# Fused lightning attention and top-1 routing: ranks in the step of the choice, GpSimd's order pinned, four gather buffers, transposed rows copied by ScalarE

## The chip, the core and the metric

The kernel runs on one core of one Trainium2 chip, in float32. The core has TensorE (PE, matrix products and transposes into PSUM), VectorE (DVE), ScalarE (ACT), GpSimd (POOL), and SyncE (SP), which here issues loads and reads. ACT, POOL and SP each have DMA queues of their own; POOL's are the ones with row indices from memory (indirect). The metric is the device time of one execution in microseconds (us), as the median of several runs.

## What is computed

Attention with a decaying state (q, k, v of 4 batches, 8 heads, 768 positions, 64 wide), its output seen as 3072 tokens of 512, then a gate that sends each token to one of 8 experts:

```python
for b in range(nb):                       # blocks of positions
    intra = einsum('bhic,bhjc->bhij', qb, kb) * Dmask
    intra = einsum('bhij,bhjd->bhid', intra, vb)
    inter = einsum('bhid,bhde->bhie', qb * lam_pow, kv_state)
    out[:, :, sl] = intra + inter
    kv_state = lam_block * kv_state + einsum('bhsd,bhse->bhde', kb * rev_pow, vb)
x = out.transpose(0, 2, 1, 3).reshape(B * S, H * D)

expert_idx = argmax(x @ w_gate, axis=1)
gate_w = softmax(x @ w_gate)[arange(N), expert_idx]
for e in range(8):                        # w1[e] is 512x1024, w2[e] 1024x512
    xe = x[expert_idx == e]
    out[expert_idx == e] = gate_w * (maximum(xe @ w1[e], 0) @ w2[e])
```

## The kernel before

**Attention.** Positions go in chunks of 128 (six, n = 0 to 5), batches in pairs, so there are 12 steps (i = 0 to 11, loop at L729); step i works on chunk i // 2. In step i the kernel *leaves* step i - 1, *enters* step i + 1 and *attends* step i. `enter` (L661) issues the loads of the next chunk on SP, transposes q and k on PE, and has POOL form kd = k x decay (L232) for the state. Attending means PE products with the state (L266), the growth of the state (cp, L299, in PSUM bank 4), products with the masked scores (L282); then `update` (L306): POOL forms sd = state x decay (L314), DVE adds cp and sd to the state st (L316). Scores of the next step follow (L242), masked by DVE into mt (L248).

`leave` (L692) turns the finished chunk into rows and gate logits on PE (tx, L324 and L326, in banks 4 to 7), ACT copies both out, and a DMA of ACT's queue writes the rows to xs in device memory. Once all four batches of a chunk are there, `choose` (L336) picks the expert of each token on DVE, as a one-hot tile oh, with running counts ohc. Tokens are thus chosen in groups: groups 0 to 4 are chunks 0 to 4 with four batches, the last chunk makes two groups of two batches. Group n is chosen in step 2n + 2.

**Lists.** `put` (L376) ranks a group's tokens within their experts by two small products on PE (L380), DVE makes slot numbers (slot_i, L389 to L394), and `store` (L395) writes one entry of four numbers for each of 128 tokens by an indirect DMA from POOL (L396); a group of four batches needs four stores. `store_places` (L678) issues up to two stores per group each time it is called. The lists are first filled with an empty entry by a 432 KB DMA from POOL (`empty_lists`, L647), out of the tile `empty`.

**Experts.** A pass works through up to 424 tokens of one expert: its list is read by SP (L421), `fetch` (L440) gathers the rows of xs by indirect DMAs from POOL into tiles xg (L445), `turn` (L468) transposes them on PE (tp, L474, banks 0 and 1) and copies them to xgT, by turns on DVE (L461) and ACT (L459). Pass 0a is the first 256 places of expert 0, taken from chunks 0 to 3 alone, so that it can start ahead of the rest; 0b is the rest of expert 0; passes 1 to 7 follow, one per other expert. Passes 0a and 0b use plain products (L484, L619). The later passes replace eight half-size products by seven, with sums of the operands: of the weights on POOL (s_q, s_k, s_v, w1t in `first_sums`; t_q, t_v, t_k, t_m in `second_sums`, L521 and L524, one pass ahead, in ring buffers of three left by the loads of q, k, v), of the tokens (t_sd, xgT, t_x, t_xT, L514 to L517) and of the hidden values (h_qsT, h_qT, h_kT, h_kd, L507 to L510) on DVE; their products are L560 and L588. The last tiles of a pass, those that don't fit the halved form, go through L619. `scatter` (L451) writes results by indirect DMAs from POOL.

**Order.** A scheduling layer places instructions on each engine's queue and sets the waits between engines; `pin` (L198) keeps an instruction in program order among those pinned. Before the change, kd, sd and the stores are not pinned. Each queue runs in order: an instruction that waits holds what stands behind it on its engine. Tiles from a pool with `bufs=n` rotate through n buffers, and a new tile waits until the last reader of the one n tiles ago is done.

Of the kernel before, what the change touches and what calls it, by code (L numbers as in the profile page):

```python
# [10 lines left out]
F32 = mybir.dt.float32  # L11
BF16 = mybir.dt.bfloat16
I32 = mybir.dt.int32
AX = mybir.AxisListType
ALU = mybir.AluOpType
# [6 lines left out]
def kernel(  # L22
# [29 lines left out]
    nc = tc.nc  # L52
    B, H, S, D = q.shape
    N, MD = out.shape
    E = moe_w_gate.shape[1]
    F = moe_w1.shape[2]
    P = 128
# [13 lines left out]
    R = N + EARLY + P  # L71
    ENTRY = 4
# [3 lines left out]
    const = ctx.enter_context(tc.tile_pool(name="const", bufs=1))  # L76
# [74 lines left out]
    for h in itertools.chain(range(0, H, 2), range(1, H, 2)):  # L151
        nc.vector.tensor_tensor_scan(
            out=decay[:, h % 2, h // 2, :], data0=lam_bc[:, h:h + 1].to_broadcast([P, C]),
            data1=ident, initial=0.0, op0=ALU.mult, op1=ALU.add)

    kdec = const.tile([P, H], F32, name="kdec")
# [28 lines left out]
    ffn = ctx.enter_context(tc.tile_pool(name="ffn", bufs=2))  # L185
# [3 lines left out]
    def bank(i, shape, name):  # L189
        return ps.tile(shape, F32, tag=f"bank{i}", name=name)  # L190
# [7 lines left out]
    def pin(inst):  # L198
        tc.keep_in_program_order(inst)
# [4 lines left out]
    def turned(src, s, t):  # L204
        for i, b in itertools.product(range(HP // 2), range(2)):
            h = s * HP + 2 * i
            pin(nc.tensor.transpose(t[:, i, b, :], src[:, b, h:h + 2, :], ident))
        return t
# [13 lines left out]
    def turn_k(m, s):  # L222
        shp = turned_shape
        tk = turned(m.k, s, bank(2 * s + 1, shp, "tk"))
        kT = work.tile(shp, F32, tag="kT", name="kT")
        nc.scalar.copy(kT, tk)
        m.kT.append(kT)
        if m.n < NSTEP - 1:
            shp = [P, 2, HP, D]
            kd = work.tile(shp, F32, tag="kd", name="kd")  # L230
            hs = slice(s * HP, (s + 1) * HP)
            nc.gpsimd.tensor_tensor(out=kd, in0=m.k[:, :, hs],  # L232
                                    in1=kdec[:, hs].unsqueeze(1).unsqueeze(3).to_broadcast(shp),
                                    op=ALU.mult)
            m.kd.append(kd)

    def score(m, s):
# [20 lines left out]
    def attend_begin(m):  # L258
        m.op = [bank(6 + b, [P, HP, C], f"op{b}") for b in range(2)]
# [46 lines left out]
    def update(m):  # L306
        if m.n < NSTEP - 1:
            to = st[:, m.b:m.b + 2]
            if m.n == 0:
                nc.vector.tensor_copy(to, m.cp)  # L310
            else:
                shp = [P, 2, HP, D]
                sd = work.tile(shp, F32, tag="sd", name="sd")
                nc.gpsimd.tensor_tensor(out=sd, in0=to,  # L314
                                        in1=sdec.unsqueeze(1).to_broadcast(shp), op=ALU.mult)
                nc.vector.tensor_add(to, m.cp, sd)  # L316

    def rows(m, b, lg):
# [84 lines left out]

        return store

    empty = ffn.tile([P, E * R // P, ENTRY], I32, tag="xg", name="empty", bufs=2)
    nc.gpsimd.memset(empty, 0)
    nc.gpsimd.memset(empty[:, :, 1], N)

# [18 lines left out]
    def at(m, t):  # L428

        w = m.widths[t]  # L430
        return m.ids[:w, t, 0:1], m.ids[:w, t, 1:2], m.list[:w, t, 2:3]
# [5 lines left out]
    def fetch(m, rows=1 + N):  # L437
        m.xg = []
        for t, w in enumerate(m.widths):
            if t % 2 == 0:  # L440
                m.xg.append(ffn.tile([P, 2, MD], F32, tag="xg", name="xg", bufs=2))
            gather(m.xg[-1][:w, t % 2, :], at(m, t)[0], rows)

    def gather(dst, idx, rows):
        nc.gpsimd.indirect_dma_start(  # L445
            out=dst, out_offset=None, in_=xs[:rows, :],
            in_offset=bass.IndirectOffsetOnAxis(ap=idx, axis=0))
# [6 lines left out]
        tc.declare_no_dep(put.ins, group="rows", reason="a token is on one list, once")  # L454
        tc.add_to_no_dep_group("rows", put.ins)

    def evac(i, dst, src):
        if i % 2:
            nc.scalar.copy(dst, src)  # L459
        else:  # L460
            nc.vector.tensor_copy(dst, src)  # L461

    def relu(i, dst, src):
        if i % 2:
            nc.scalar.activation(dst, src, ACT.Relu)
        else:
            nc.vector.tensor_scalar_max(dst, src, 0.0)

    def turn(m, pin=lambda inst: inst):
        m.xgT = ffn.tile([P, DC, m.n], F32, tag="xgT", name="xgT", bufs=1)  # L470
        for dc in range(DC):
            tp = bank(next(tp_banks), [P, m.n], "tp")
            for t, w in enumerate(m.widths):
                pin(nc.tensor.transpose(tp[:, t * P:t * P + w],  # L474
                                        m.xg[t // 2][:w, t % 2, dc * P:(dc + 1) * P],
                                        ident[:w, :w]))
            evac(dc, m.xgT[:, dc, :], tp)

    def hidden(m, w1t):
        m.hT = ffn.tile([P, FC, m.n], F32, tag="hT", name="hT", bufs=1)  # L480
# [154 lines left out]
    sdec = const.tile([P, HP, 1], F32, name="sdec")  # L635
# [25 lines left out]
    def enter(n, b):  # L661
        if n + 1 < NSTEP:
            loaded[n + 1, b] = load(n + 1, b)
        if (n, b) == (NSTEP - 2, B - 2):
            weights.append(load_weights(0))
        m = SimpleNamespace(n=n, b=b, qT=[], qsT=[], kT=[], kd=[], mt=[], xT=[])
        m.q, m.k, m.v = loaded[n, b]

        for s, turn_one in (((0, turn_q), (1, turn_q), (0, turn_k), (1, turn_k)) if not (n or b)
                            else ((0, turn_q), (0, turn_k), (1, turn_q), (1, turn_k))):  # L670
            turn_one(m, s)
        return m

    chosen = []

    waiting = []

    def store_places():  # L678
        for group, store, i in waiting:
            for j in range(i, min(i + 2, len(group[1]))):  # L680
                store(j)
        done = [group for group, _, i in waiting if i + 2 >= len(group[1])]
        waiting[:] = [(group, store, i + 2) for group, store, i in waiting
                      if i + 2 < len(group[1])]
        if any(group[:2] == early for group in done):
            start_early()

    def give_places(group):

        waiting.append((group, put(*group), 0))  # L690

    def leave(m):  # L692
        for b in range(2):
            n, bs = group_of[m.n, m.b + b]
            i = bs.index(m.b + b)
            if i == 0:
                lgs[0] = small.tile([P, len(bs), DC // 2, E], F32, tag="lg", name="lg")
            rows(m, b, lgs[0][:, i])
            if i == len(bs) - 1:

                chosen.append(choose(n, bs, lgs[0]))
# [5 lines left out]
    def start_early():  # L707

        nc.vector.tensor_scalar(out=skip, in0=had, scalar1=-1.0, scalar2=float(EARLY),
                                op0=ALU.mult, op1=ALU.add)  # L710
        nc.vector.tensor_scalar_max(skip, skip, 0.0)
        base[0] = const.tile([P, E], F32, name="ebase_late")
        nc.vector.tensor_copy(base[0], ebase)
        nc.vector.tensor_add(base[0][:, 0:1], base[0][:, 0:1], skip)
        m = make_pass(0, 0, EARLY, "0a")
        fetch(m, 1 + (NSTEP - 2) * B * C)
        passes.append(m)
# [7 lines left out]
    for j, u in itertools.product(range(2), range(2)):  # L725
        pin(nc.scalar.dma_start(
            out=back[(u ^ j) * D:((u ^ j) + 1) * D, :, P + j * E:P + (j + 1) * E],
            in_=by_chunk[j, u]))
    for i in range(len(order)):  # L729
        due = chosen.pop() if chosen else None  # L730
        if last:
            leave(last)

        ahead = enter(*order[i + 1]) if 0 < i < len(order) - 1 else None
        attend_begin(cur)
        if cur.n < NSTEP - 1:
            attend_states(cur, 0)
            grow(cur)
            attend(cur)
        else:  # L740

            attend(cur)
            attend_states(cur, 0)
            if ahead:
                for s in range(2):
                    score(ahead, s)
            else:
                turn(passes[0], pin)
        attend_states(cur, 1)
        to_sbuf(cur)  # L750
        if i == 0:
            ahead = enter(*order[1])
        update(cur)
        if i == 0:
            later_decays()

        if due:
            give_places(due)
        store_places()
        if i == 2:  # L760
            empty_lists()
        if ahead and cur.n < NSTEP - 1:
            for s in range(2):
                score(ahead, s)
        last, cur = cur, ahead
    give_places(chosen.pop())
    store_places()
    leave(last)
    give_places(chosen.pop())
    store_places()  # L770


    cnt = bank(7, [P, E], "cnt")
# [10 lines left out]
    shp = [P, NR, NR]  # L784
    more = small.tile(shp, F32, tag="more", name="more")
    nc.vector.tensor_tensor(out=more, in0=rkey.unsqueeze(1).to_broadcast(shp),
                            in1=rkey.unsqueeze(2).to_broadcast(shp), op=ALU.is_gt)
# [5 lines left out]
                            op=ALU.is_equal)  # L793
# [23 lines left out]
    for m in passes[1:3]:  # L817
        fetch(m)
# [30 lines left out]
    with tc.If(most > 0):  # L849
        for i in range(E):  # L850
            tiles = nc.values_load(beyond[0:1, i:i + 1], min_val=0, max_val=MORE[i])
            with tc.If(tiles > 0):
# [4 lines left out]
                with tc.For_i(0, tiles, 1) as r:  # L857
                    m = SimpleNamespace(n=P, widths=[P])
# [3 lines left out]
                        out=m.list[:, 0, :], in_=pick(by_e, e)[bass.ds(r * P + CAPS[i], P), :])  # L862
# [32 lines left out]
```

## Time and profile before

| | |
|---|---|
| time, median of 5 runs | 474.12 us (473.69 to 475.21) |
| the profiled execution's own time | 472.26 us |
| its span | 470.5 us |
| POOL waiting for transposes ahead of a gather (L445 behind L474) | 64.7 us in 6 waits |
| POOL: mean of one store (L396), one gather (L445) | 0.97 us, 1.08 us |
| ACT, DVE: copy of transposed rows, 128x368 | 0.47 us, 0.53 us |
| DMA over the span | 154 GB/s; 11 to 117 us nearly full |
| granted clock of TensorE, whole span | 0.992 |

The profile is of one execution. "Span" is the time from its first to its last instruction; the execution's own time lies 1.76 us above it. An engine's busy time is that of its instructions; waits are told by who released them. The chain of waits follows the execution back from its end: at each piece, what ended the wait before it. In a line of the timeline stand start, duration, engine, source line, operation, output and inputs, shape, count, and, in brackets, the engine's idle time before it and what ended it. The attention runs from 0 to about 131 us, pass 0a from 124.7 to 161, passes 1 to 7 from 171 to 464.

### The profile page before, as it was taken

The page shows a single profiled execution, that of the slowest core. Times are in us where ns is not written, and L with a number is a line of the kernel's source. Part 1 is how long each engine was busy: PE and PEld are TensorE (multiplying, and loading weights), DVE is VectorE, ACT ScalarE, POOL GpSimd, SP SyncE. Part 2 cuts the span into 40 slices and gives each one's busy share as a digit, 9 for nine tenths or more (in the row PEclk, how much of TensorE's full clock was granted, in tenths as well). Part 3 has the DMA queues.
Part 4 walks back from the last instruction along what each step waited for, and adds up shares of the span by engine and source line. Part 5 has one row for each costly group of instructions (what it writes and reads, how often), then busy time and mean ns, then how long its engine had stood idle before and what let it go on. Part 6 is the DMA issues. An engine that isn't in the chain of part 4 may idle for free.

```text
span 470.5 us, 8624 instructions
## 1 busy us (share of the span) xinstructions
PE 451.0 (96%) x3447; PEld 374.8 (80%) x3447; DVE 221.3 (47%) x495; ACT 125.7 (27%) x323; POOL 247.1 (53%) x190
## 2 busy tenths in 40 slices
PE   4989999999699999999999999999999999999994
PEld 4889899999586576956994898599689689779863
DVE  2764859676450133452345436434624623753421
ACT  3454445544330111222131222013112212211210
POOL 5323635423154849949806951992695497711001
PEclk9999999999989999999999999999999999999998
DMA  9999999999216667160506152451624516001001
GB/s 177 226 274 246 230 242 223 243 311 300 91 47 219 211 218 254 55 250 30 203 21 246 34 217 76 169 185 64 242 76 170 213 48 226 1 20 45 1 17 52
DMA packets 99840, 72.60 MB, mean 154 GB/s; under 512 B 81235, under 2 KB 81239, under 8 KB 99792
## 3 DMA queue, kind: packets, MB, share of 16 engines
q1 hardware_dynamic: 90608, 52.49, 41.4%
q0 software_dynamic: 5008, 13.16, 7.8%
q10 hardware_dynamic: 4176, 6.31, 4.1%
q8 instruction: 29, 0.48, 0.5%
q14 instruction: 19, 0.16, 0.1%
HBM read 58.88 MB, written 13.16 MB: 153 GB/s over the span
## 4 chain that ended last, share of the span: by engine, by line
PE 70%; issue 2%; DVE 1%; DMA 1%; POOL 1%; POOLq 0%; ACT 0%
PE p L560 27%; PE p L588 18%; PE po L619 17%; PE ph L484 4%; PE tp L474 3%; DMA xg<-xs,list_0a 1%; POOL slots L396 0%; DVE h_qsT L507 0%; PE op L266 0%; DVE hT L569 0%; PE tx L326 0%; PE tx L324 0%; DVE xgT L461 0%; POOLq L848 0%; ACT hT L571 0%
## 5 line engine op out<-in xcount | busy, mean ns | idle before, releaser
L619 PE MATMUL po<-w2t,hT 128*128 128x512 f32 (+5 forms) x224 | 81.0, 596 | 0.0
L445 POOL DMA_INDIRECT xg<-xs,list x24 | 25.8, 1075 | 70.2 <-PE tp L474 64.7
L619 PEld LDWEIGHTS po<-w2t,hT 128*128 128x128 f32 (+5 forms) x224 | 30.5, 162 | 38.2 <-issue 37.9
L571 ACT ACTIVATE hT<-hT 128x408 f32<-128x408 f32 (+4 forms) x56 | 29.5, 527 | 86.7 <-DVE hT L569 86.7
L451 POOL DMA_INDIRECT out_dram<-o,list x24 | 23.7, 989 | 50.9 <-DVE o L625 27.7
L560 PE MATMUL p<-xgT,w1t 128*128 128x204 f32 (+4 forms) x224 | 41.5, 328 | 0.0
L232 POOL TENSOR_TENSOR kd<-k_in,kdec 128x512 f32<-128x512 f32 x20 | 20.5, 1048 | 36.5 <-PE cp L299 22.4
L396 POOL DMA_INDIRECT slots<-entry,slot_i x24 | 23.3, 972 | 29.5 <-DVE slot_i L394 14.4
L560 PEld LDWEIGHTS p<-xgT,w1t 128*128 128x128 f32 x224 | 37.6, 190 | 1.2 <-issue 0.9
L248 DVE TENSOR_TENSOR mt<-sp,decay 128x512 f32<-128x512 f32 x48 | 29.8, 683 | 10.3 <-PE sp L242 10.1
L600 DVE SCALAR_TENSOR_TENSOR o<-p,list,o 128x256 f32<-128x256 f32 x28 | 13.6, 484 | 32.9 <-PE p L588 17.0
L588 PE MATMUL p<-w2t,hT 128*128 128x256 f32 x112 | 26.8, 382 | 0.0
L588 PEld LDWEIGHTS p<-w2t,hT 128*128 128x128 f32 x112 | 21.0, 190 | 7.0 <-issue 4.5
L242 PE MATMUL sp<-qT,kT 64*128 64x128 f32 x384 | 25.8, 286 | 0.0
L242 PEld LDWEIGHTS sp<-qT,kT 64*128 64x128 f32 x384 | 23.5, 195 | 1.8 <-issue 0.9
L282 PE MATMUL op<-mt,v_in 128*64 128x128 f32 x384 | 23.3, 274 | 0.4 <-ACT x L331 0.4
L474 PEld LDWEIGHTS tp<-ident,xg 128*128 128x128 f32 (+3 forms) x112 | 13.4, 141 | 12.6 <-issue 3.6
L484 PE MATMUL ph<-xgT,w1t 128*128 128x256 f32 (+1 forms) x128 | 23.3, 339 | 0.0
L569 DVE TENSOR_TENSOR hT<-p,u_qsT 128x408 f32<-128x408 f32 (+4 forms) x28 | 15.7, 561 | 15.8 <-PE p L560 15.8
L474 PE MATMUL tp<-ident,xg 128*128 128x128 f32 (+3 forms) x112 | 18.6, 277 | 3.7 <-DMA xg<-xs,list_0a 2.4
L291 ACT COPY xT<-op 128x512 f32<-128x512 f32 x24 | 12.9, 589 | 34.6 <-PE op L266 27.5
L282 PEld LDWEIGHTS op<-mt,v_in 128*64 128x64 f32 x384 | 20.8, 137 | 1.0 <-ACT x L331 0.6
(164 smaller groups left out, 934.6 us busy)
## 6 DMA issues: line engine op xcount, KB each, us to landing
w1t<-in_moe_w_dram SPq DMA_DIRECT2D x8, 2048.0 KB, 7.8
w2t<-in_moe_w_dram SPq DMA_DIRECT2D x8, 2048.0 KB, 8.2
v_in<-in_v_dram SPq DMA_DIRECT2D x12, 512.0 KB, 7.8
xs<-x ACTq DMA_DIRECT2D x24, 256.0 KB, 5.0
q_in<-in_q_dram SPq DMA_DIRECT2D x11, 512.0 KB, 7.8
k_in<-in_k_dram SPq DMA_DIRECT2D x11, 512.0 KB, 8.0
q_in<-in_q_dram SPq DMA_DIRECT2D x2, 256.0 KB, 4.4
k_in<-in_k_dram SPq DMA_DIRECT2D x2, 256.0 KB, 5.6
```

What stands on the lines that cost most here:

```text
L242: pin(nc.tensor.matmul(sp[u][:, i, b, :], lhsT=m.kT[s][halves[u], i, b, :], rhs=m.qT[s][halves[u], i, b, :], start=(i == 0 and b == 0), st ...
L248: nc.vector.tensor_mul(mt[:, u], sp[u], decay[:, u, s * HP // 2:(s + 1) * HP // 2].unsqueeze(2).to_broadcast(shp))
L282: pin(nc.tensor.matmul(out_at(m, b, u, hp), lhsT=m.v[:, b, 2 * hp + u, :], rhs=m.mt[hp // 2][:, u, hp % 2, b, :], start=(m.n in (0, NSTEP ...
L396: put = nc.gpsimd.indirect_dma_start(out=slots, out_offset=bass.IndirectOffsetOnAxis(ap=slot_i[:, i:i + 1], axis=0), in_=entry[:, n, bs[i] ...
L445: nc.gpsimd.indirect_dma_start(out=dst, out_offset=None, in_=xs[:rows, :], in_offset=bass.IndirectOffsetOnAxis(ap=idx, axis=0))
L451: put = nc.gpsimd.indirect_dma_start(out=out, out_offset=bass.IndirectOffsetOnAxis(ap=idx, axis=0), in_=src, in_offset=None, bounds_check= ...
L474: pin(nc.tensor.transpose(tp[:, t * P:t * P + w], m.xg[t // 2][:w, t % 2, dc * P:(dc + 1) * P], ident[:w, :w]))
L484: nc.tensor.matmul(ph, lhsT=w1t[:, dc, fc * P:(fc + 1) * P], rhs=m.xgT[:, dc, :], start=(dc == 0), stop=(dc == DC - 1))
L560: nc.tensor.matmul(p[:, i, :], lhsT=lhs[:, dc, (c + i) * P:(c + i + 1) * P], rhs=rhs[:, dc, :], start=(dc == 0), stop=(dc == DH - 1))
L571: nc.scalar.activation(outs[i][k], outs[i][k], ACT.Relu)
L588: nc.tensor.matmul(p, lhsT=lhs[:, fc, :], rhs=rhs[:, fc, :], start=(fc == 0), stop=(fc == FC // 2 - 1))
L619: nc.tensor.matmul(po[part], lhsT=m.hT[:, fc, t * P:t * P + w], rhs=w2t[:, fc, :], start=(i < k), stop=(i >= FC - k), skip_group_check=True)
```

## The change

1. The places of a group are given in the step in which it is chosen (`give_places` right after the step's `update`) and not one step later. Group n's ranks thus go to the end of step 2n + 2, its first two stores to that step, its other two to the next one; the early pass 0a is started at the end of step 9.
2. kd, sd and the stores are pinned, and a one-element-wide memset of a new tile `between` stands between the two stores of a pair. On POOL's queue each step then reads: two kd, sd, store, memset, store.
3. The empty lists are written at the end of step 1 and not of step 2. On POOL's queue that DMA stands behind six kd; before, behind four kd and one sd.
4. Tiles `xg` (and `empty`) rotate through four buffers instead of two.
5. `turn` copies transposed rows on ACT alone; `evac`, which alternated, goes.

As built, the order of POOL's queue in passes 1 to 6 changes too. Before: s_k, w1t, s_q, s_v, two scatters, the gathers of the pass after next, t_q, t_v, t_k, t_m, scatters. After: s_k, w1t, s_q, s_v, two scatters, t_q, t_v, t_k, t_m, the gathers, scatters. PE's order is the same but for the moved ranks, for the transposes of 0a, where the first product of the pass now stands among them, and for a few products around the last choice. On DVE the 18 copies of the passes are gone, on ACT they stand with the 18 it had: two copies, one rectification, two copies in each later pass.

```diff
@@ turn_k, update: kd and sd
-            nc.gpsimd.tensor_tensor(out=kd, in0=m.k[:, :, hs],
-                                    in1=kdec[:, hs].unsqueeze(1).unsqueeze(3).to_broadcast(shp),
-                                    op=ALU.mult)
+            pin(nc.gpsimd.tensor_tensor(
+                out=kd, in0=m.k[:, :, hs],
+                in1=kdec[:, hs].unsqueeze(1).unsqueeze(3).to_broadcast(shp), op=ALU.mult))
...
-                nc.gpsimd.tensor_tensor(out=sd, in0=to,
-                                        in1=sdec.unsqueeze(1).to_broadcast(shp), op=ALU.mult)
+                pin(nc.gpsimd.tensor_tensor(
+                    out=sd, in0=to, in1=sdec.unsqueeze(1).to_broadcast(shp), op=ALU.mult))
@@ gather buffers
-    empty = ffn.tile([P, E * R // P, ENTRY], I32, tag="xg", name="empty", bufs=2)
+    empty = ffn.tile([P, E * R // P, ENTRY], I32, tag="xg", name="empty", bufs=4)
...
-                m.xg.append(ffn.tile([P, 2, MD], F32, tag="xg", name="xg", bufs=2))
+                m.xg.append(ffn.tile([P, 2, MD], F32, tag="xg", name="xg", bufs=4))
@@ turn
-            evac(dc, m.xgT[:, dc, :], tp)
+            nc.scalar.copy(m.xgT[:, dc, :], tp)
@@ store_places
-    def store_places():
+    between = const.tile([P, 1], F32, name="between")
+
+    def store_places(pin=pin):
         for group, store, i in waiting:
             for j in range(i, min(i + 2, len(group[1]))):
-                store(j)
+                if j > i:
+                    pin(nc.gpsimd.memset(between, 0.0))
+                pin(store(j))
@@ the loop over the steps
     for i in range(len(order)):
-        due = chosen.pop() if chosen else None
         if last:
             leave(last)
...
-        if due:
-            give_places(due)
+        if chosen:
+            give_places(chosen.pop())
         store_places()
-        if i == 2:
+        if i == 1:
             empty_lists()
...
-    give_places(chosen.pop())
-    store_places()
     leave(last)
     give_places(chosen.pop())
-    store_places()
+    store_places(lambda inst: inst)
```

More of the change, by code (lines that the diff above doesn't have):

```diff
@@ L455, in scatter @@
         tc.add_to_no_dep_group("rows", put.ins)
[L457 to L461, printed above, removed]
     def relu(i, dst, src):
```

## The prediction

> **What bounds the kernel now.** I read the page's summary first, then the chain of waits in order of time, then the timeline at each place where the chain leaves TensorE (PE).
>
> ```profile
> span 470.5 us, 8624 instructions
> ...
> PE 451.0 (96%) x3447; PEld 374.8 (80%) x3447; DVE 221.3 (47%) x495; ACT 125.7 (27%) x323; POOL 247.1 (53%) x190
> ```
>
> PE is busy for 451.0 of 470.5 us, and the change takes no matmul away. So it can gain only where PE idles or runs at a lower clock. By stretches of the span, PE idles 7.8 us up to 117 us (mostly the first loads), 3.9 between 117 and 137, nothing between 137 and 405, 1.1 between 405 and 410, and 6.6 after that (the tail). The chain names two of these.
>
> ```profile
> 114.58 6.06 issue
> 120.64 0.28 POOL xg L445
> 120.92 1.01 issue
> 121.93 5.43 DMA xg<-xs,list_0a
> ...
> 137.08 10.47 PE ph L484 x48
> ...
> 406.23 1.83 DVE h_qsT L507
> 408.06 0.45 DVE hT L569
> 408.51 0.45 DVE xgT L461
> ```
>
> The first is the gather of the early tokens of expert 0 (list_0a): stores of the places, list, gather, and only then PE's transposes (tp, L474), which could have begun at 124.72 and begin at 127.40. The second is a copy of transposed rows that stands behind a sum on VectorE (DVE). The timeline shows what the gather waits for, and the table by stage what the wait does to the clock (its last three columns are granted clock, DMA share and GB/s):
>
> ```profile
> 113.62 0.96 POOL L396 DMA_INDIRECT slots<-entry,slot_i  x1 [0.30 <-issue]
> 118.18 0.37 SPq L421 DMA_DIRECT2D list_0a<-slots  x1
> ```
>
> ```profile
> 126.00:128.00 2.00, 0.55 (x3) 0.31 (x3) 0.23 (x1) 0.02 (x1) 0.00 (x0) 1.00 0.04 14
> 128.00:130.00 2.00, 1.75 (x20) 1.28 (x20) 0.61 (x2) 0.73 (x2) 0.00 (x0) 0.62 0.00 0
> 130.00:132.00 2.00, 2.00 (x16) 1.38 (x9) 1.02 (x7) 1.07 (x2) 0.00 (x0) 0.53 0.00 0
> ```
>
> The list is read 4.56 us after the last store was issued. After the idle stretch PE runs 4 us at 0.62 and 0.53 of its clock: 2 x 0.38 + 2 x 0.47 = 1.7 us more lost.
>
> **Places one step earlier, in twos.** A step of the attention lasts 9.87 us (19.75 for two, between GpSimd's kd at 75.82 and 95.57). Group 3's ranks move from step 9 (107.75) to the end of step 8, where PE ends the state products at about 97.9. DVE then has st (98.17 to 98.84), four small operations that took 0.9 us from 108.63 to 109.51, and slot_i stands at about 100. GpSimd (POOL) issues two stores at 1.27 each to 102.5, then sd (1.04), then two more to 106. At 4.56 to 6.3 us (the median landing of these stores) they have landed by 110 to 112. The list read goes to SP's queue behind v_in and the two 2 MB weight loads, which keep the DMAs full until 116 (share 0.64 in 115 to 116, 0.10 after that); so I take the list at 112 to 116.3. Two gathers at 1.29 and 5.43 us from the second's issue give rows at 119 to 123.3. PE asks at 124.72: the wait goes, with 1.4 us to spare at the late end.
>
> What PE then does from 124.72 on, at full clock: eight transposes, the copies now all on ScalarE (ACT) at 0.37 each, so that the third waits for the first copy: 1.7 us; state products 0.6; rank 0.1; two pairs of ph records 0.87 (0.218 a record, 10.47 / 48); 16 tx records 1.85; five pairs of ph 2.2; the final choice, whose DVE chain reached its rank 2.6 us after the last tx, adds 0.3; one and 23 more pairs 10.5. Sum 18.2 us, an end of ph at 142.9 in place of 147.55. **Gain 4.6 us** (2.7 idle, 1.7 clock, the rest small). All places, lists and loads behind it come earlier too; PE does not wait for them before 405.
>
> [...]
>
> **The pinned order, memsets, the empty lists.** sd moves behind the next kd pair: POOL has kd from 85.39 to 87.43, then sd to 88.47, while st on DVE began at 88.19. So st is 0.29 later each step and must be done before tx takes bank 4 at 90.12; it would end at 89.2. Nothing on PE. In return sd no longer runs beside the place product:
>
> ```profile
> 88.96 1.04 POOL L314 TENSOR_TENSOR sd<-st,sdec 128x512 f32<-128x512 f32 x1 [1.54 <-DVE st L316]
> 89.01 1.04 DVE L390 TENSOR_TENSOR place<-place,oh 128x32 f32<-128x32 f32 x1
> ```
>
> L390 takes 0.17 to 0.19 elsewhere. With ranks in even steps, mt there begins about 1.9 us after sp, against 2.25 in this odd step, which cost PE nothing. Twelve memsets on POOL at 0.10 (its 128x1 memsets) lie in the 0.30 gap between two stores. POOL needs 2.08 + 1.04 + 2.5 = 5.6 of 9.87 us, so kd(9) starts at 95.3 in place of 95.57. If this cover were gone, 0.3 a step for 8 steps is 2.4 us lost. The empty lists (432 KB) go from behind four kd to behind six, from 19.93 to about 27.5. k_in holds PE for 0.47 us at 23 and 1.25 at 32; the same bytes move before 33 with the DMAs full (share 1.14), so I take 0, between a gain of 1.25 and a loss of 1.7 (432 KB at 254 GB/s).
>
> **Four buffers.** POOL's gathers waited 64.7 us for transposes in all:
>
> ```profile
> POOL xg L445 <- PE tp L474: 64.7, 6, 15.7
> ```
>
> That wait also held back the sums t_q, t_v, t_k, t_m, which stand behind a gather in POOL's queue (375.11 in the pass before last). In the changed order they stand ahead of the gathers, as they do now in the last pass alone. There t_v waits for its buffer until 405.16, and POOL runs beside DVE:
>
> ```profile
> 405.16 2.35 POOL L524 TENSOR_TENSOR t_v<-w2t 128x1024 f32<-128x1024 f32 x1 [2.63 <-PE p L560]
> 407.47 2.80 POOL L524 TENSOR_TENSOR t_k<-w2t,t_q 128x1024 f32<-128x1024 f32 x1
> 410.35 2.52 POOL L524 TENSOR_TENSOR t_m<-w2t,t_k 128x1024 f32<-128x1024 f32 x1
> 410.58 2.83 DVE L508 TENSOR_TENSOR h_qT<-hT 128x512 f32<-128x512 f32 x1
> 413.78 0.67 DVE L509 TENSOR_TENSOR h_kT<-h_qT,hT 128x512 f32<-128x512 f32 x1
> ```
>
> h_qsT takes 1.83 us and h_qT 2.83 where the pass before has 0.69. DVE operations that read PSUM (0.53 to 0.75) are as fast as ever. So the change brings this collision to passes 2 to 5. What counts is the date: the second product needs h_kT 1.9 us after the L588 group starts. In the last pass h_kT was done at 414.45 against 417.3, with PE 1.1 late; without that delay and with about 0.9 us of xgT copies taken off DVE ahead of it, about 413.6 against 416.2. 2.6 us to spare: cost 0 per pass, at most 1.1 (what the last pass pays now), 4.4 for four.
>
> [...]
>
> **Copies on ScalarE.** 18 copies of 0.3 to 0.6 us leave DVE; ACT is 27% busy. In a fast pass ACT takes two at 0.47 right after the first transposes, while PE has 0.87 us of po; the third and fourth transposes find their banks free. In the last pass PE no longer waits for DVE behind h_qsT: **gain 1.1 us** (bounds 0 and 1.1).
>
> **Sum.** 4.6 + 1.1 = 5.7 us off the profiled execution, 472.26 to 466.6. That execution lies 1.86 under the median of the runs, 474.12; the same cut gives **468.4**. Likeliest case alone: 466.2 to 470.
>
> **Rivals.** (1) The gather is still late: SP reads the list only behind the weights and the rows land near 127. For it: the full DMAs until 116. Against it: they are idle from 117 to 122. PE keeps up to 2.4 us: 474.12 - 5.7 + 2.4 = 470.8. (2) The pinned order costs the attention what the routing gains: st, held by sd, is late for bank 4, or a load for PE at 33, 0.3 to 0.6 in each of 8 to 10 steps, some 5 us in all. For it: st's slack is 0.9. Against: only 0.29 is used. About 473.5, no change to speak of. (3) Slower: in passes 2 to 6 the sums of POOL and DVE collide so that h_kT misses its date. One further POOL sum of 2.35 us in that stretch uses the 2.6, a second one lands on PE. At 2.35 a pass for five passes, 11.8 lost against 4.6 won: 481.3. It decides from 2.6 us more delay of DVE than the last pass shows; t_q, released 5 us before t_v, speaks against it.
>
> **How the numbers follow.** Forecast 0.60, rival 1 0.17, rival 2 0.10, rival 3 0.13. This kernel's measurement can tell 0.2%, about 0.95 us, from no change. Faster: the forecast, rival 1 and a third of rival 2, 0.80; same 0.06; slower: rival 3 and the rest, 0.14. The range runs from 466.0 (the early loads' 1.25 and more gained) to 472.8, which takes in rival 1 and part of 2.
>
> **What would show it.** Right: list_0a read before 117, the gather issued before 118, no wait of L474, granted clock 1.00 from 117 to 137; h_qsT and h_qT of 1.8 to 2.8 us in passes 2 to 6 with PE unbroken between 137 and the tail; tp without a wait in the last pass. Wrong: PE waiting at L588 for h_kT or at L619 for a bank; PE waiting at tx or rank in the attention; a list read later than 118.

## The result, and the profile after

The changed kernel takes 471.17 us (median of 50 runs) against 473.90 for the kernel before (92 runs): a ratio of 0.9948, 95% interval 0.9936 to 0.9960. It is faster, by some 2.5 us, less than half of the 5.7 that the forecast summed up. The profiled execution took 470.44 us.

The page's summary for the changed kernel, span and busy times:

```profile
span 468.7 us, 8634 instructions
...
PE 450.3 (96%) x3447; PEld 374.9 (80%) x3447; DVE 237.3 (51%) x477; ACT 132.4 (28%) x341; POOL 252.2 (54%) x202
```

PE does what it did; DVE is busier by 16 us although 18 copies have left it; the collision with POOL has spread, as foreseen (h_qsT takes 1.63 us in the mean where it took 0.86, h_qT 2.52 where it took 0.99). The chain of waits around the early gather (start, us, what):

```profile
104.33 6.88 DMA slots<-entry,slot_i
...
111.27 8.18 DMA list_0a<-slots
...
120.27 0.28 POOL xg L445
...
121.57 5.58 DMA xg<-xs,list_0a
...
127.19 0.34 PE tp L468
```

The places are stored 9.3 us sooner (the last at 104.33, before at 113.62), and the rows arrive at 127.15, before at 127.36. All that was won at the stores is lost at one step, the read of the list, 8.18 us for 4 KB. SP's timeline says where the first part of it went:

```profile
111.27 4.76 SPq L421 DMA_DIRECT2D list_0a<-slots  x1
```

That is the time of issuing alone, 0.37 us in the kernel before. Ahead of it in SP's queue stand the two 2 MB loads of expert 0's weights (w1t, w2t) and a 512 KB load of v (v_in). The DMA view gives the time from issue to landing (last column):

```profile
w1t<-in_moe_w_dram SPq DMA_DIRECT2D x1, 2048.0 KB, 13.2
w2t<-in_moe_w_dram SPq DMA_DIRECT2D x1, 2048.0 KB, 18.1
v_in<-in_v_dram SPq DMA_DIRECT2D x1, 512.0 KB, 20.3
list_0a<-slots SPq DMA_DIRECT2D x1, 4.0 KB, 8.2
```

The three loads were issued at 94.87, 98.34 and 99.01. So w1t had landed (108.1) before the read's issue began at 111.27; the issue ended at 116.03, shortly before w2t landed (116.4), and the list landed at 119.45, right behind v_in (119.3). So PE waits as before, and pays with its clock as before. PE's timeline, and the table by stage (the columns after the five engines are granted clock, DMA share, GB/s):

```profile
125.94 0.33 PE L468 MATMUL tp<-ident,xg 128*128 128x128 f32 x1 [1.89 <-DMA xg<-xs,list_0a]
127.19 0.55 PE L468 MATMUL tp<-ident,xg 128*128 128x128 f32 x3 [0.93 <-DMA xg<-xs,list_0a]
```

```profile
126.00:128.00 2.00, 0.83 (x5) 0.40 (x5) 0.00 (x0) 0.44 (x2) 1.44 (x3) 0.97 0.04 10
128.00:130.00 2.00, 2.00 (x10) 1.37 (x14) 0.00 (x0) 0.59 (x3) 0.00 (x0) 0.50 0.02 1
130.00:132.00 2.00, 2.00 (x22) 1.59 (x23) 0.68 (x4) 1.28 (x3) 0.00 (x0) 0.67 0.00 0
```

At 0.97, 0.50 and 0.67 of the clock 2 x (0.03 + 0.50 + 0.33) = 1.7 us go, the same as before.

What was won lies in the experts. In the last pass, DVE's and PE's timelines:

```profile
405.64 1.84 DVE L502 TENSOR_TENSOR h_qsT<-hT 128x512 f32<-128x512 f32 x1 [0.58 <-ACT hT L566]
407.85 2.23 DVE L509 TENSOR_TENSOR t_sd<-xgT 128x360 f32<-128x360 f32 x1
410.00 2.83 DVE L503 TENSOR_TENSOR h_qT<-hT 128x512 f32<-128x512 f32 x1
412.87 0.69 DVE L504 TENSOR_TENSOR h_kT<-h_qT,hT 128x512 f32<-128x512 f32 x1
```

```profile
407.05 0.79 PE L468 MATMUL tp<-ident,xg 128*128 128x128 f32 x6
407.68 6.18 PE L614 MATMUL po<-w2t,hT 128*112 128x512 f32 x14
413.69 1.89 PE L583 MATMUL p<-w2t,hT 128*128 128x256 f32 x8
415.42 1.89 PE L583 MATMUL p<-t_k,h_kT 128*128 128x256 f32 x8
```

The transposes at 407.05 have no bracket, so no wait, where 1.09 us stood before; h_kT is done at 413.56 and asked for at 415.42. The last pass's L583 begins 1.9 us sooner than in the profile of before (415.59): 0.36 of it come from the early pass, 1.09 from this wait and about 0.5 from small ones (0.15 to 0.17 us in each of passes 3 to 5), less 0.26 that pass 0b loses; some 0.2 I can't place. The two profiles lie 1.8 us apart in their spans, the runs 2.5. The rest isn't accounted for by a run. Part of it may be clock: where both kernels ran in one group (c1, below), the mean granted clock of the runs is 0.9925 for the changed kernel (12 runs) and 0.9900 for the kernel before (28), which over 470 us is some 1.2 us, an estimate.

### The profile page after: what moved, and what is told of

Same layout as the page of the kernel before. It is cut to its first block, busy times and chain, and to the rows that moved or that the text cites. A ratio compares the mean times of both kernels' runs of the same rounds, so it can differ in the third digit from the quotient of the medians.

```text
span 468.7 us, 8634 instructions
## 1 busy us (share of the span) xinstructions
PE 450.3 (96%) x3447; PEld 374.9 (80%) x3447; DVE 237.3 (51%) x477; ACT 132.4 (28%) x341; POOL 252.2 (54%) x202
## 4 chain that ended last, share of the span: by engine, by line
PE 85%; DMA 6%; SPq 3%; issue 2%; POOL 2%; DVE 0%; ACT 0%; POOLq 0%
PE p L555 28%; PE p L583 18%; PE po L614 17%; PE ph L479 5%; PE tp L468 3%; SPq L93 3%; PE sp L242 3%; PE op L282 3%; DMA k_in<-in_k_dram 2%; PE op L266 2%; DMA list_0a<-slots 2%; PE tx L324 2%; PE cp L299 2%; DMA slots<-entry,slot_i 1%; PE tx L326 1%
## 5 line engine op out<-in xcount | busy, mean ns | idle before, releaser
L519 POOL TENSOR_TENSOR t_q<-w2t 128x1024 f32<-128x1024 f32 x7 | 16.5, 2358 | 39.9 <-PE p L555 39.9
L583 PE MATMUL p<-w2t,hT 128*128 128x256 f32 x112 | 26.8, 382 | 0.0
L583 PEld LDWEIGHTS p<-w2t,hT 128*128 128x128 f32 x112 | 21.0, 190 | 7.0 <-issue 4.5
L519 POOL TENSOR_TENSOR t_v<-w2t 128x1024 f32<-128x1024 f32 x7 | 16.5, 2361 | 17.2 <-PE p L555 17.2
L468 PEld LDWEIGHTS tp<-ident,xg 128*128 128x128 f32 (+2 forms) x112 | 13.7, 142 | 11.7 <-issue 5.9
```

Source lines behind the costliest of these rows:

```text
L468: pin(nc.tensor.transpose(tp[:, t * P:t * P + w], m.xg[t // 2][:w, t % 2, dc * P:(dc + 1) * P], ident[:w, :w]))
L519: return nc.gpsimd.tensor_tensor(out=o, in0=x, in1=y, op=ALU.subtract)
L583: nc.tensor.matmul(p, lhsT=lhs[:, fc, :], rhs=rhs[:, fc, :], start=(fc == 0), stop=(fc == FC // 2 - 1))
```

## The experiments

The experiments ran in three groups, two on one chip and the third (e2b, e9, e10, c2) on another; each is compared with runs of the kernel before from its own group, whose medians were 474.86, 475.19 and 473.59 us. Line numbers are those of each kernel.

**The second weight load behind the list (e2, again as e2b).** To the changed kernel, shortened:

```diff
 start_early:
         m = make_pass(0, 0, EARLY, "0a")          # the read of the list, pinned
+        weights[0] = weights[0], load_w2(0, pin)  # was issued with w1t, in step 9's enter
         fetch(m, 1 + (NSTEP - 2) * B * C)
```

> The changed kernel with one edit: the 2 MB load of expert 0's second weights stands behind the read of the early list in SP's queue, not ahead of it. Theory A: 2 MB less ahead of the read, and stores that land sooner (4.6 instead of 6.9 us after their issue); list by 113, rows by 120, no wait at L468, time 466.5 to 467.5; the weights then land by 125, PE needs them at 147. Rival B (full engines whatever the order) expects 470 to 471. Rival D (the attention's loads or the rows' writes suffer from the later weights): a new wait of PE before 124, over 471.

469.54 us, ratio 0.9888 (0.9856 to 0.9920). The same kernel again, on the other chip:

> The kernel of e2 (the changed kernel with expert 0's second weight load behind the list read) once more. If the early gather was the whole of what the change missed, it is again 4.5 to 6 us faster than before (ratio 0.987 to 0.9905) with list_0a issued in under 1 us, no wait of the early tp on the gather and a granted clock of 1.00 from 117 to 137. If the first result was a lucky chip state, the ratio is that of the changed kernel, 0.993 to 0.997.

467.03 us, ratio 0.9873 (0.9852 to 0.9893): 6 us under before, more than twice the gain of the change. SP's timeline, POOL's, and the table by stage of that run:

```profile
113.36 0.37 SPq L424 DMA_DIRECT2D list_0a<-slots  x1
113.78 0.50 SPq L179 DMA_DIRECT2D w2t<-in_moe_w_dram  x1
```

```profile
116.22 0.99 POOL L450 DMA_INDIRECT xg<-xs,list_0a  x1 [8.91 <-DMA list_0a<-slots]
```

```profile
126.00:128.00 2.00, 1.75 (x22) 1.21 (x14) 0.00 (x0) 1.18 (x4) 0.96 (x2) 1.00 0.07 10
128.00:130.00 2.00, 2.00 (x27) 1.60 (x26) 0.69 (x4) 1.45 (x3) 0.00 (x0) 1.00 0.00 0
130.00:132.00 2.00, 2.00 (x18) 1.98 (x17) 0.00 (x0) 1.18 (x6) 1.75 (x3) 1.00 0.02 1
```

Issued in 0.37 us, landed 1.9 us after its start (the gather starts 2.9 us after it), no wait of PE on the gather and the clock at 1.00 from 117 to 137. This settles which step failed: the date of the list's read, with w2t issued ahead of it. The edit takes w2t out of SP's queue ahead of the read and out of the DMAs at the same time, so it doesn't tell which of the two held the read.

**The list read through POOL's queue (e1).** `nc.sync.dma_start` became `nc.gpsimd.dma_start` for list_0a alone.

> The changed kernel with one edit: the list of pass 0a is read by a DMA from GpSimd's queue, not SP's. Theory A (the read is late because it stands in SP's queue behind 4.5 MB of weights and v_in; its issue took 4.76 us there, others take 0.37): it is issued at about 111 as before, lands by 115.5, gathers at about 116, rows by 122.5, no wait of the transposes L468, clock 1.00 from 117 to 137, end of ph near 143, time 466.5 to 467.5. Rival B (the DMA engines are full until 116, so any queue is as slow): list at 118 to 119, time as the changed kernel, 471. Rival C (the list is early but the gathered rows now compete with the loads): list at 115, rows at 124 to 126, time 468.5 to 470.

468.91 us, ratio 0.9899 (0.9863 to 0.9936). But POOL's timeline shows that the list was not quick there either:

```profile
114.17 0.79 POOL L422 DMA_DIRECT2D list_0a<-slots  x1 [7.21 <-DMA slots<-entry,slot_i]
120.72 1.00 POOL L446 DMA_INDIRECT xg<-xs,list_0a  x1 [5.76 <-DMA v_in<-in_v_dram]
```

Without the queue ahead of it the list still took 6.3 us to land while the DMAs were full (share 1.11 from 114 to 118, 0.74 from 118 to 120); in nearly idle ones, in e10, it took 2.06 us. PE did not wait for the rows, which came at 126.28, since it had lost 2.2 us in the attention and asked only then. So the profile doesn't show why the runs are fast, and the case for the list rests on the experiment before. That another queue didn't make the list quick speaks for full DMAs as part of the cause.

**Only the weight load moved, in the kernel before (e10).** The same edit as in the first experiment, with the places stored as late as before.

> The kernel before with only the second weight load moved behind the list read: the list is read from a free queue but the places are stored as late as before (last store issued at 113.6). Theory: the stores set the date, the list is read at 117 to 118.5 and the gather issued at 119.5 to 121, PE still waits 1.5 to 3 us and loses clock: ratio 0.998 to 1.002. Rival: the queue alone was the limit, ratio 0.9895 to 0.992. Other rival: the second weights now come too late for the early pass's second product: slower, ratio over 1.003.

474.40 us, ratio 1.0015 (0.9992 to 1.0038): nothing. The stores set the date of the list, as the theory said, but its rows came even later, for another reason. The chain of waits:

```profile
113.08 2.45 DMA slots<-entry,slot_i
...
115.59 2.06 DMA list_0a<-slots
...
119.76 8.23 DMA xg<-xs,list_0a
...
128.04 0.49 PE tp L479
```

Stores and list now pass through DMAs that are nearly idle from 114 on (0 to 12 GB/s until 117), in 2.45 and 2.06 us; but then the 2 MB start, and the gather takes 8.23 us behind them (5.43 before). The load that is moved out of the list's way gets into the gather's way. Only with the places a step sooner (in e2b the second gather is issued at 117.52 and lands 6.3 us later) are the rows there before PE asks. The change's earlier places were necessary, and by themselves not enough.

**The order and the weight load, without the other parts (e9).** Pinned order, places in twos, w2t behind the list; two buffers and the old copies (shortened; the lines show what goes back against the changed kernel):

```diff
-    name="xg", bufs=4        # and the tile empty
+    name="xg", bufs=2
-            nc.scalar.copy(m.xgT[:, dc, :], tp)
+            if dc % 2:
+                nc.scalar.copy(m.xgT[:, dc, :], tp)
+            else:
+                nc.vector.tensor_copy(m.xgT[:, dc, :], tp)
```

> The kernel before with GpSimd's new order and the second weight load behind the list read, but two buffers and the old copies: the routing part alone, with its list in time. Theory: the routing part is worth what was forecast for it, 4.6 us (4 to 5), ratio 0.9895 to 0.9915, and the last pass still waits 1.1 us at tp for DVE behind h_qsT. Rival: the order alone costs something in the attention (e11 measured +0.7), so 2.5 to 3.5 us are left, ratio 0.9925 to 0.995.

467.75 us, ratio 0.9889 (0.9870 to 0.9908): 5.3 us, with an interval of 4.4 to 6.2. So the routing with its list in time is worth about the 4.6 of the forecast or a little more. In this profile the last product into ph of the early pass ends at 142.69; the forecast had 142.9. PE's waits still show the last pass's 1.1:

```profile
PE tp L473 <- DVE xgT L480: 1.4, 2, 1.1
```

**The order alone (e11)**, the same without the move of w2t:

> The kernel before with the other parts of the change but two buffers and the old copies: GpSimd's order pinned, places stored in twos one step earlier, empty lists one step earlier. Theory: the early gather comes only 0.4 us sooner, and the attention ends 0.6 us sooner because of the early loads: 0.9 to 1.4 us faster, ratio 0.997 to 0.998; the list lands at 118 to 120. Rival: the order brings nothing, 0.9995 to 1.0005. Other rival: the order is worth 2.5 us or more by itself, ratio 0.9948 or less, and the copies nothing.

475.85 us, ratio 1.0024 (0.9996 to 1.0051). List issued at 111.4 in 5.79 us, gather at 120.34, PE waits 3.0 us. The forecast of 0.9 to 1.4 us lies outside the interval, so it missed; without the weight load's move the order brings nothing that can be measured. Against e9 (the two ratios are from different groups, each with its own runs of before), a single load's place in SP's queue is worth some 1.3% of the time.

**The copies alone (e3)**, in the kernel before:

> The kernel before with one part of the change: all copies of transposed rows on ScalarE. Theory: PE no longer waits 1.1 us behind h_qsT in the last pass and 0.15 us in each of passes 3 to 5, and waits 0.26 us more in the pass 0b: 1.1 to 1.5 us faster than before, ratio 0.9968 to 0.9977. Rival: the copies are the whole gain of the change, ratio 0.994 to 0.9955. Other rival: nothing, 0.999 to 1.001, because the last pass waits for h_kT next. The profile should show the second tp group of the last pass without a wait on DVE.

474.47 us, ratio 0.9980 (0.9957 to 1.0004). The last pass waits no more on DVE. The ratio lies just above the first theory's 0.9968 to 0.9977, but the interval reaches from 2 us faster to nothing; from the two kernels with the list in time, 0.9873 with copies and buffers and 0.9889 without, about 0.7 us, but with intervals that overlap. So no pair of runs shows a gain of the copies clear of noise; their profiles show the wait gone. This run's profile also has two waits of PE that the profile of before has not, 1.08 us for DVE's hT at 143.46 and 0.82 us for a gather at 173.18; why they came is open.

**Two buffers (e5)**, in the changed kernel (only the first pair of lines of the diff above):

> The changed kernel with one part undone: two gather buffers instead of four, copies on ACT. Theory: the four buffers bring PE nothing; GpSimd's sums stand behind the gathers again and collide with DVE's in the last pass alone; 471 plus or minus 0.7. Rival: the earlier gathers and sums are worth something to PE: 472.5 or more.

472.91 us, ratio 0.9956 (0.9926 to 0.9986), like the change itself. Taken by the microseconds alone, the rival's 472.5 or more came; but before ran at 474.86 in this group, so I go by the ratio. The engines' busy time from 137 to 405 us (PE, PEld, DVE, ACT, POOL), changed kernel, then two buffers:

```profile
137.00:405.00 268.00, 267.74 (x1345) 216.59 (x1344) 133.27 (x203) 58.55 (x123) 179.89 (x104) 1.00 0.44 150
```

```profile
137.00:405.00 268.00, 267.73 (x1342) 215.96 (x1341) 104.83 (x213) 58.53 (x124) 174.77 (x103) 1.00 0.43 151
```

Four buffers cost DVE 28 us, in operations that run beside POOL's sums (in the profiles of before and after, h_qT takes 0.68 to 0.69 us without one beside it and 2.83 with one), and change PE by nothing.

**The old copies (e4)**, in the changed kernel (the second pair):

> The changed kernel with one part undone: the copies of transposed rows alternate again between DVE and ACT. Theory: with four gather buffers the sums of GpSimd and DVE collide in passes 2 to 6, and a DVE copy behind a slowed sum holds PE in each: 1.1 us (the last pass of the kernel before) times five, less 0.3 to 0.5 that the ACT copies cost in pass 0b and the early pass, so 475 to 476.5. Rival: only the last pass has that wait: about 472.

478.58 us, ratio 1.0086 (1.0059 to 1.0113), slower than before, and more than I expected. PE's waits, and one of four like places in the chain of waits:

```profile
PE tp L468 <- DVE xgT L475: 4.9, 6, 1.1
```

```profile
333.62 0.57 DVE hT L567
334.21 0.53 ACT hT L569
334.77 1.81 DVE h_qsT L505
336.57 0.47 DVE hT L567
337.04 0.46 DVE xgT L475
337.55 0.74 PE tp L468 x5
```

With four buffers, POOL runs beside DVE in the later passes, h_qsT takes 1.8 us where it takes 0.69 in the kernel before, and the copy queued behind it lets PE wait: 1.0 to 1.1 us in four passes, 0.3 in two. The copies on ACT make the buffers harmless; without these, the buffers made the kernel slower (1.0086 against 1.0024 for the order alone, on one chip). In this profile 2.7 us more are lost to the hold of ACT that is told at the end.

**The changed kernel again (c1), and the kernel before again (c2)**, for their profiles on the two chips:

> The changed kernel itself, beside the kernel before on the same chip. In the profiles of the first four experiments ScalarE's second rows transfer near 92 to 97 us held ScalarE's queue for 2.9 to 4.0 us, and PE lost 1.5 to 4.1 us at the matmuls behind the fence copy (op <- ACT fence); the profiles of before and after that were read first show neither. Theory A: the hold comes from loads that land late in some executions, whatever the kernel, so this profile shows it too (1 us or more at op <- ACT fence between 85 and 110 us) and the ratio to before stays at 0.993 to 0.997. Theory B: it came from the edits of those experiments, so this profile shows under 0.3 us there. Under both, if the list of the early tokens is late for good, it lands at 118 to 120 and PE waits 2 to 3 us for the early gather, with a granted clock of 0.5 to 0.7 for about 4 us after it.

473.76 us, ratio 0.9973 (0.9945 to 1.0001); list issued at 113.7 in 5.50 us, gather at 122.25, later than expected, PE waits 2.3 us. At op behind the fence PE lost 0.6 us: neither theory's bound is met. (The fence, L276, is ACT's copy of a few numbers out of an output bank; PE's next products into op wait for it.)

> The kernel before itself, for its profile on this chip: PE waits 2.2 to 3 us for the early gather and runs at a granted clock of 0.5 to 0.8 for 4 us after it; if ScalarE's hold at the rows transfer belongs to the executions and not to the changed order, PE loses here, too, some 0.5 us or more at op <- ACT fence between 85 and 110 us when the other profiles of this call do.

List issued at 120.3, gather at 122.73, PE waits 2.7 us and runs at 0.50 to 0.72 until 135; nothing lost at the fence.

**Rows written by POOL (e8)**, with w2t behind the list:

```diff
-        nc.scalar.dma_start(out=xs[r0:r0 + C, :], in_=x)
+        pin(nc.gpsimd.dma_start(out=xs[r0:r0 + C, :], in_=x))   # the last one not pinned
```

> The changed kernel with two edits: expert 0's second weight load behind the list read (as in e2), and the rows of the attention's output written to HBM by transfers that GpSimd issues, in place of ScalarE, pinned where they stand. Theory: ScalarE's queue no longer stands at the second rows transfer, so its copies of the next step's k and the fence come in time and PE loses nothing at op <- ACT fence: 466 to 468, 1.5 to 3.5 us under e2's 469.5. Rival: GpSimd now stands at the rows (x is ready only 2 to 3 us before the next kd), kd or a store comes late and PE waits at cp or rank: 470 to 474. Other rival: it is the loads themselves that are late, and PE waits for k_in in the same place: 469 to 470.

472.81 us, ratio 0.9938 (0.9913 to 0.9962), worse than with ACT's queue. PE's waits:

```profile
PE op L285 <- ACT x L334: 5.7, 1, 5.7
```

The rival held, at another place: POOL stands at the early gather until 117.6, behind the list (landed at 116.8); the rows queued behind it keep their buffer of x, ACT can't fill the next one and PE stops for 5.7 us. The loss at the fence was gone.

## Why the forecast was right in its sign and wrong in its size

**The step that failed** is "so I take the list at 112 to 116.3". The stores came as worked out (issued from 99.5 to 104.3; landed at 111.2, forecast 110 to 112). For the list I took the time at which the DMAs fall idle, 116, as the late bound and let the gather follow at once. In fact the read was held in its own issue until 116.0, while w2t, ahead of it in SP's queue, was still under way, and then took another 3.4 us to land, right behind v_in: 119.45. My late bound lacked the read's own landing, and rows at 123.3 at the latest became 127.15. The profile of before had rows for both. The gather starts 2.46 us after the list's issue (118.18 to 120.64), so the landing lies inside that. And the lists of the later passes are small reads behind two 2 MB loads in the same queue:

```profile
144.37 0.38 SPq L174 DMA_DIRECT2D w1t<-in_moe_w_dram  x1
144.93 0.37 SPq L176 DMA_DIRECT2D w2t<-in_moe_w_dram  x1
145.49 15.82 SPq L421 DMA_DIRECT2D list<-slots  x6
```

Six reads of 8 KB hold SP's queue for 15.82 us, 3.63 of it the issue of the first and 4.99 that of the second. I did not use this line; with it, an issue of 3.6 to 5 us could have been expected.

**The case that came** is rival 1, at 470.8 against 471.17 measured. Its condition, the list read behind the weights, was named, and I gave it 0.17 because the DMAs are idle from 117 to 122; the list needed just that stretch. That its number is so near is in part luck. Rival 1 left 2.2 of the 4.6 us to the routing, the clock's 1.7 among them; in the profile the wait was 2.82 us, the clock cost 1.7 again, and the early pass's ph ended 0.36 us sooner (147.19 in place of 147.55). The runs' gain above the profiles' 1.8 us, which no run accounts for, makes up for part of the difference.

**The size of the routing term**, 4.6, was about right for a list in time: 5.3 us in the kernel with the order and the weight load alone (interval 4.4 to 6.2). That it measured somewhat more, though not clear of noise, would fit the clock: in the profile of before the wait cost 1.7 us of clock, in the second one (c2), in stretches of 2 us from 127 on, 2 x (0.28 + 0.50 + 0.50 + 0.43) = 3.4. Two readings in the forecast's working were slightly off and decide nothing: the first transpose did run at 124.72, so the idle time was 2.35 us and not 2.7, and the terms from 124.72 on add up to 18.1, not 18.2.

**The clock.** The drop came here behind a wait of 1.89 us, a transpose of 0.33 and a wait of 0.93, and all ten profiles with a wait of 2.3 us or more between 117 and 137 show it; in the four without, the clock stood at 1.00 from 117 to 137. So the row of the kernel before, with 1.7 us lost behind one wait of 2.35, was the one to sum by. The stretch without any product other than transposes is longer than the wait: from the end of op at 124.05 to ph at 128.47, 4.4 us, and 4.3 in the kernel before. No run here tells whether the drop goes with the wait or with this stretch.

**The copies**, 1.1 in the last pass: the wait is gone as forecast, with some 0.5 more from small waits of the other passes, which I had not counted, and 0.26 us lost in pass 0b, where the first copy stands on ACT behind an output (o, 0.69 us). The whole effect measured some 0.7 us, which isn't clear of noise: the intervals of the two kernels with the list in time overlap, and nothing lies inside the interval of the run that had the copies alone.

**The buffers**, nothing: right, and the collision spread as foreseen, with PE unbroken. h_kT was ready 1.9 us ahead of its product (2.6 forecast). What I priced as a bound, 1.1 a pass, is what the old copies would have made of it: 4.9 us of waits. It was the copies, not the slack of h_kT, that decided. So rival 3 did not come, and with the old copies the loss comes by another way than I gave it.

**The pinned order, memsets and empty lists**, nothing in the attention of the changed kernel's first profile: no wait at tx or rank on st, memsets of 0.11 us inside the gaps, PE's waits for k_in 1.9 us in all in place of 2.1. Rival 2 did not come by the way it was priced; a loss in the attention of another kind, seen in some executions, is told at the end.

## What to carry to other kernels

Here a small read that decided a date stood behind large loads in its queue, and moving one of them was worth more than the whole change. Follow such a read from issue to landing, and count both the queue ahead of it and the DMAs' load. Moving a producer earlier pays only up to the next thing that is late; here the earlier places and the later weight load were each worth nothing measurable alone and some 5 us together. When an engine gets more room to run ahead (more buffers), ask which operations of another engine then run beside its own, what they cost there (here 2.83 us for h_qT in place of 0.69), and what stands behind them in that engine's queue on the critical path.

## What the runs showed that was not expected

**Issuing can block.** A DMA issue that takes 0.37 us on a free queue took 4.76 to 5.88 in all five profiles of the new order with both weight loads ahead of it on the same queue. In the changed kernel's profile w1t had landed at 108.1, before the issue began at 111.27, and the issue ended at 116.03, 0.4 us before w2t landed.

**A hold of ACT in the attention.** In six of nine profiles of kernels with the new order PE lost 0.6 to 3.6 us between 85 and 100 us, at the products behind ACT's fence copy, because ACT stood at the second transfer of rows, whose wait ends, by the profile, when an earlier load of k lands. ACT's timeline in the kernel with two buffers:

```profile
92.38 0.63 ACT L214 COPY qT<-tq 128x512 f32<-128x512 f32 x1
94.31 0.33 ACTq L334 DMA_DIRECT2D xs<-x  x1
94.68 0.23 ACT L346 ACTIVATE ex<-sh 128x32 f32<-128x32 f32 x1 [1.67 <-DMA k_in<-in_k_dram]
```

The kernel with the order alone differs from it only in copies after the attention, and lost nothing there; the changed kernel itself lost nothing in its first profile and 0.6 us in its second. So it varies between executions of the same instructions. Four profiles with the old order show none of it; whether the new order makes it likelier stays open, and what a kernel without it would take was not found, since rows written by POOL cost more than the hold.

**The price of one wait varies.** In the two profiles of the kernel before, with the same instructions, PE waited 2.35 us for the early gather in one (behind the first transpose) and 2.40 + 0.31 us in the other (around it); once 1.7 us of clock were lost and once 3.4. All ten profiles with a wait of this size fall on one of these two prices: from 117 to 137 the granted clock is 0.91 in six (waits of 2.3 to 2.9 us) and 0.83 in four (2.7 to 5.7 us), that is some 1.8 or 3.4 us lost, and nothing between.
